# Clustered attention and two FFNs on one core: small attention steps rewritten to read PSUM, the planner's costs re-set, and the first transfers put in another order

## The chip, the cores and the metric

One core of one Trainium2 chip runs the whole program. The metric is device time in microseconds (us) of one execution, lower is better. A measurement of this kernel can tell about 1% (8 us) from no change.

## The reference

```python
def _attn_ref(q, k, v, centroids):              # B,H,S,D = 2,8,768,64; 16 clusters
    q_n = q / (norm(q) + 1e-06); k_n = ...; c_n = ...
    q_assign = argmax(einsum('bhsd,hcd->bhsc', q_n, c_n), axis=-1)   # k_assign alike
    mask = q_assign[:, :, :, None] == k_assign[:, :, None, :]
    scores = where(mask, scale * q @ k.T, -1000000000.0)
    scores = scores - max(scores, axis=-1, keepdims=True)
    attn = exp(scores); attn = attn / (sum(attn) + 1e-09)
    return attn @ v
# x = attention output as (1536 tokens, 512)
def _moe_ref(x, w_in, w_out, alpha):            # d_ff = 2048
    h = x @ w_in
    return (maximum(h, 0) + alpha * minimum(h, 0)) @ w_out
def _moe2_ref(x, w_in, w_out, a, b):
    h = x @ w_in
    P = a[0] + a[1]*h + a[2]*h**2 + a[3]*h**3
    Q = 1.0 + abs(b[0])*abs(h) + abs(b[1])*h**2
    return (P / (Q + 1e-6)) @ w_out
```

The FFN weights arrive as float64 and are rebuilt as float32 on the chip. A query whose cluster holds no key gets the mean of v.

## The kernel before

The attention works on 16 heads in 8 pairs. Everything is kept as two float32 or float16 parts, a high one and a remainder ("hi" and "lo"), so that the products are accurate.

For a pair, `ph_T` transposes q and k (L523; ACT writes hi, VectorE subtracts lo, L528 and L530), `ph_logits`, `ph_lt` and `ph_oht` find the cluster of each row and make a one-hot matrix (L592 writes it). `operands1` and `operands2` then copy the parts of a head into the operand tiles `op1` and `op2` by DMA (L615, L618, L621 and L629, L633).

For a head, `max_chunk` forms nine 512-column score tiles in PSUM (L659), each reduced to row maxima on VectorE (L665). `m_chain` takes the maximum of the parts (L674), makes `nm` from it (L677, VectorE, SBUF to SBUF), flags rows without a key (`nh`, L679, GpSimd), transposes nm (L682), negates it (L684) and sends it by DMA as a row of `op1` (L686). `st_chunk` computes the scores again with that row subtracted (L705, L706) and ACT takes the exponential (L710). `p_split` turns the result into float16: hi is a cast (the helper `copy`, L414 on ACT or L416 on GpSimd), lo is a subtraction of two SBUF tiles (L722). `pv_tile` multiplies by v (L790 to L792, 18 matmuls for a tile of 128 queries, 6 tiles for a head), and `pv_fin` divides: four small or middle VectorE steps L807, L809, L810 and L812, and L814, which overwrites rows without a key with the mean of v, from SBUF into SBUF. `x_T` transposes the pair's output into x.

`v_split` does a pair's v once: a scale from the sum of squares (L733, L740, L745 to L755), the mean of v (reduce L737, L742), then hi (L765, L767) and lo (L770).

The FFNs follow in 96 steps of 12 matmuls of 512 columns for h (L1033) and 12 for y (L1102). `w_prep` loads and rebuilds weights (L973, L976, L996 to L1018; L1009 and L1016 on GpSimd). Its first weights are prepared while the attention still runs.

The order of all instructions is written by a planner, `Sched`. Each `op` has a list of alternatives (engine, cost in us, a bias, and for some a hold of a port that the planner treats as shared by VectorE and GpSimd), the tiles it reads and writes, a priority `SC.t`, and an earliest time `after`. `run` walks in planned time, always starts what can start first, and picks the alternative with the earliest planned end plus bias. `BIAS["DVE"]` is added to every VectorE alternative of an op that has more than one. The planned order becomes the order in each engine's in-order queue; all DMAs go through SyncE's queue. `nb(n)` is the planned duration of a transfer of n bytes, `first` the earliest planned times of the first loads. The lo of `p_split`, L722, has these two alternatives, and in the kernel before all 96 went to GpSimd:

```python
        op([but(dve2(S), -0.1715), but(pool2(S), -0.0503)],
           lambda e: e.tensor_sub(pt_.v[:, 1, :], src(), pt_.v[:, 0, :]),
```

With S = 768 `dve2` costs 0.866 and `pool2` 1.783.

Of the kernel before, what the change touches and what calls it, by code (L numbers as in the profile page):

```python
# [253 lines left out]
def clustered_attention__then__ffn_prelu__then__ffn_rational(  # L254
# [471 lines left out]
    vmean, vinv = {}, {}  # L726

    def v_split(j):
        raw, d = raws["v", j], vs[j % 2]
        am, vr, vm_, ps = SC.buf("am"), SC.buf("vr"), SC.buf("vmean"), SC.buf("o", "v")  # L730
        junk = SC.buf("junk")
        for h in range(2):
            op(act_s(384, 2), lambda e, h=h: e.activation(  # L733
                junk.v.rearrange("p (t d) -> p t d", t=T), raw.v[:, h], ACTF.Square,
                accum_out=vr.v[:, 2 * D + h:2 * D + h + 1]),
               r=[raw], w=[(vr, h), junk])
# [5 lines left out]
        op([(ACT, 0.17), (DVE, 0.2)], lambda e: (e.mul(vm_.v, ps.v[:, :2 * D], 1.0 / S)  # L742
           if e is nc.scalar else e.tensor_scalar(vm_.v, ps.v[:, :2 * D], 1.0 / S, None,
                                                  op0=ALU.mult)), r=[ps], w=[vm_])
        op((DVE, 0.1), lambda e: e.tensor_scalar(  # L745
            am.v[:, 2:4], ps.v[:, 2 * D:2 * D + 2], 2.0 ** -120, None, op0=ALU.max),
           r=[ps], w=[am])
        op((DVE, 0.1), lambda e: e.tensor_scalar(
            am.v[:, 2:4].bitcast(U32), am.v[:, 2:4].bitcast(U32), 1, 0x7F800000,
            op0=ALU.logical_shift_right, op1=ALU.bitwise_and), r=[am], w=[am])  # L750
# [1 line left out]
        op((POOL, 0.17), lambda e: e.tensor_scalar(
            am.v[:, 2:4], am.v[:, 2:4], 2.0 ** 50, 0.0, op0=ALU.mult, op1=ALU.add),
           r=[am], w=[am])
        op((POOL, 0.17), lambda e: e.tensor_scalar(  # L755
            am.v[:, 0:2], am.v[:, 0:2], 2.0 ** -50, 0.0, op0=ALU.mult, op1=ALU.add),
           r=[am], w=[am])
# [415 lines left out]
```

## Time and profile before

| | us |
|---|---|
| median of 3 runs | 821.07 (818.24 to 824.56) |
| the profiled execution, its own time | 825.44 |
| its span, first to last instruction | 823.4 |
| mean granted TensorE clock | 0.965 |
| busy: TensorE 768.9 (93%), VectorE 606.6 (74%), ScalarE 570.4 (69%), GpSimd 596.2 (72%) | |

In the rows PE is TensorE (PEld its weight loads), DVE VectorE, ACT ScalarE, POOL GpSimd, SPq the queue of SyncE, from which DMAs are issued. "a<-b" says what is written and what is read; arenas are the two large SBUF areas, `bank` is PSUM. A time in brackets with an arrow is idle time of the engine before the instruction and what ended it. A busy PE is not PE at its peak, since matmuls are pipelined.

### The profile page before, as it was taken

To read this page: it belongs to the slowest core of one execution; us is meant where nothing else is said; L and a number is where in the kernel's file an instruction comes from. 1 tells how busy PE (TensorE), PEld (TensorE's weight loads), DVE (VectorE), ACT (ScalarE), POOL (GpSimd) and SP (SyncE) were. 2 spreads that over 40 slices of the span, in tenths; PEclk is the share of its full clock that TensorE was granted. 3 is DMA by queue.
4 is the path that set the end of the run, shared out by engine and by line. 5 is a ranking of instruction groups with operands and counts; after the bars stand their busy time and mean duration, and the time that the engine had idled before them with its cause. 6 is when DMAs were issued, how large, how long until landed. Compare 5 with 4: busy or idle time off the path is not lost.

```text
span 823.4 us, 13646 instructions
## 1 busy us (share of the span) xinstructions
PE 768.9 (93%) x5103; PEld 636.6 (77%) x5103; DVE 606.6 (74%) x884; ACT 570.4 (69%) x1002; POOL 596.2 (72%) x496
## 2 busy tenths in 40 slices
PE   7888888999878579999999999999999999999997
PEld 6667767878757458888888888888888888888885
DVE  5695979899786867865455365358889889987775
ACT  3377869888877757765564465579989788767662
POOL 4077659778677999987575476689889789877443
PEclk9888989999989889999999999999999999999999
DMA  8653737667435222333131032021111111000012
GB/s 166 138 102 84 154 72 167 129 132 165 109 70 168 86 95 81 111 117 102 52 103 52 30 99 78 26 67 62 52 42 61 52 51 52 1 0 1 2 52 102
DMA packets 57858, 67.56 MB, mean 82 GB/s; under 512 B 27232, under 2 KB 46272, under 8 KB 57792
## 3 DMA queue, kind: packets, MB, share of 16 engines
q1 hardware_dynamic: 57792, 66.69, 31.2%
q8 instruction: 40, 0.66, 0.3%
q14 instruction: 26, 0.21, 0.1%
HBM read 43.04 MB, written 3.15 MB: 56 GB/s over the span
## 4 chain that ended last, share of the span: by engine, by line
PE 61%; DVE 1%; POOL 1%; issue 1%; ACT 0%; DVEq 0%; POOLq 0%
PE bank L1102 31%; PE bank L1033 30%; DVE arena_p L1044 0%; POOL arena_p L1061 0%; POOL arena_r L1079 0%; POOL arena_p L722 0%; DVE arena_p L1121 0%; DVE rc L810 0%; PE bank L792 0%; DVE arena_p L1006 0%; PE bank L790 0%; PE bank L791 0%; PE bank L830 0%; DVE bank L1044 0%; ACT arena_r L414 0%
## 5 line engine op out<-in xcount | busy, mean ns | idle before, releaser
L1102 PE MATMUL bank<-arena_r 128*128 128x512 f32 x1152 | 278.5, 390 | 8.8 <-ACT arena_r L414 8.4
L1033 PE MATMUL bank<-x,arena_r 128*128 128x512 f32 x1152 | 278.5, 391 | 0.4 <-POOL arena_r L1016 0.4
L1102 PEld LDWEIGHTS bank<-arena_r 128*128 128x128 f32 x1152 | 216.3, 188 | 55.4 <-ACT arena_r L414 9.2
L1033 PEld LDWEIGHTS bank<-x,arena_r 128*128 128x128 f32 x1152 | 216.7, 188 | 46.1 <-POOL arena_r L1016 1.1
L722 POOL TENSOR_TENSOR arena_p<-arena_p 128x768 f16<-128x768 f32 x96 | 162.8, 1716 | 31.1 <-ACT arena_p L414 27.3
L1079 POOL TENSOR_TENSOR arena_r<-arena_p,arena_r 128x512 fp32r<-128x512 f32 x96 | 133.4, 1390 | 52.2 <-ACT arena_r L414 41.9
L414 ACT CAST arena_r<-arena_p 128x512 fp32r<-128x512 f32 x133 | 80.8, 620 | 48.8 <-DVE arena_p L1044 29.4
L665 DVE TENSOR_REDUCE mp<-bank 128x1 f32<-128x512 f32 x144 | 92.0, 680 | 25.9 <-PE bank L659 25.6
L1044 DVE SCALAR_TENSOR_TENSOR arena_p<-arena_p,nal 128x512 f32<-128x512 f32 x48 | 54.2, 1130 | 70.2 <-ACT arena_p L1047 70.1
L1016 POOL TENSOR_TENSOR arena_r<-arena_p,arena_r 128x512 fp32r<-128x512 f32 x64 | 88.6, 1388 | 19.4 <-ACT arena_r L414 18.6
L1009 POOL TENSOR_TENSOR arena_p<-arena_p 128x512 int32<-128x512 int32 x64 | 90.6, 1418 | 11.1 <-ACT arena_p L1002 7.1
L710 ACT ACTIVATE arena_p<-bank 128x512 f32<-128x512 f32 x144 | 79.7, 594 | 23.0 <-PE bank L706 14.6
L1004 DVE TENSOR_SCALAR arena_p<-arena_p 128x512 uint32<-128x512 uint32 x64 | 61.4, 961 | 41.3 <-ACT arena_p L996 41.3
L705 PE MATMUL bank<-arena_r 128*128 128x512 f32 x192 | 70.1, 382 | 14.2 <-DVE mp L665 6.0
L1061 POOL TENSOR_TENSOR arena_p<-arena_p 128x512 f32<-128x512 f32 x48 | 62.7, 1309 | 26.7 <-ACT arena_p L1058 26.6
L1006 DVE SCALAR_TENSOR_TENSOR arena_p<-arena_p 128x512 uint32<-128x512 uint32 x64 | 75.2, 1174 | 1.1
L414 ACT CAST arena_p<-arena_p 128x768 f16<-128x768 f32 x93 | 74.5, 838 | 0.3
L706 PE MATMUL bank<-arena_r 128*128 128x512 f32 x192 | 65.0, 352 | 0.0
L790 PE MATMUL bank<-arena_p 128*128 128x65 f16 x576 | 63.4, 199 | 1.1 <-DVE arena_p L812 1.1
L1044 DVE SCALAR_TENSOR_TENSOR arena_p<-arena_p,cq,bank 128x512 f32<-128x512 f32 x48 | 35.8, 745 | 38.9 <-ACT bank L1069 31.8
L792 PE MATMUL bank<-arena_p 128*128 128x65 f16 x576 | 62.5, 198 | 1.3 <-POOL arena_p L722 1.1
L791 PE MATMUL bank<-arena_p 128*128 128x64 f16 x576 | 62.7, 197 | 0.0
(121 smaller groups left out, 1247.2 us busy)
## 6 DMA issues: line engine op xcount, KB each, us to landing
arena_p<-in_moe_w_in SPq DMA_DIRECT2D x32, 512.0 KB, 3.6
arena_p<-in_moe_w_out SPq DMA_DIRECT2D x32, 512.0 KB
arena_r<-arena_r SPq DMA_DIRECT2D x24, 384.0 KB, 4.0
arena_r<-arena_r SPq DMA_DIRECT2D x24, 192.0 KB, 5.4
arena_p<-in_q SPq DMA_DIRECT2D x8, 384.0 KB, 5.3
arena_p<-in_k SPq DMA_DIRECT2D x8, 384.0 KB, 7.0
arena_r<-x SPq DMA_DIRECT2D x8, 384.0 KB, 9.6
arena_p<-in_v SPq DMA_DIRECT2D x8, 384.0 KB
```

The source lines that it names most:

```text
L414: e.copy(o_, i_)
L665: op(dvep(CH), lambda e: e.reduce_max(mp.v[:, n0:n0 + np_], ps.v.rearrange("p (a k) -> p a k", a=np_), axis=AX.X), r=[ps], w=[(mp, c)])
L705: e.matmul(o_, lhsT=b_.v[:, 1, ks], rhs=b_.v[:, 0, lo:hi], start=True, stop=False)
L710: op(act_p(CH), lambda e: e.activation(p32.v.rearrange("p a s -> p (a s)")[:, cc * CH:(cc + 1) * CH], ps.v, ACTF.Exp, scale=scale), r=[ps] ...
L722: lambda e: e.tensor_sub(pt_.v[:, 1, :], src(), pt_.v[:, 0, :]),
L1006: op(dve2(N), lambda e, d0=d0, hi=hi: e.scalar_tensor_tensor(u(d0), hi(), 0x80000000, u(d0), op0=ALU.bitwise_and, op1=ALU.bitwise_or), r=[ ...
L1009: op(pool2(N), lambda e, d0=d0, d1=d1: e.tensor_tensor(n32(d0), n32(d0), n32(d1), op=ALU.add), r=[d0, d1], w=[d0])
L1016: lambda e, wt=wt, pick=pick, src=src: e.tensor_tensor(pick(wt.v)[:, 1], src(), f32(pick(wt.v)[:, 0]), op=ALU.subtract),
L1033: e.matmul(ps.v, lhsT=wi.v[:, wi_, kk, :], rhs=x[kk][:, xi, cols], start=n == 0, stop=n == 3 * KD - 1)
L1044: lambda e: e.scalar_tensor_tensor(o_.v, a_.v, sc, b_.v, op0=p0, op1=p1))
L1079: op([dve2(N), pool2(N)], lambda e: e.tensor_tensor(gg.v[:, 1, :], G.v, f32(gg.v[:, 0, :]), op=ALU.subtract), r=[G, (gg, 0)], w=[(gg, 1)])
L1102: e.matmul(ps.v, lhsT=lhsT, rhs=rhs, start=first and wi_ == gi == 0, stop=last and gi == 1)
```

## The change

- `m_chain`: L677 and the tile nm go. The padding column that each tile's maxima get holds -BIG/2, so L674 itself gives the limited maximum; the transpose takes mx, and the constant is added where the transposed row is negated.
- `v_split`: the mean of v goes (L737, L742, L745); the scale comes from one VectorE step that reads PSUM, one on GpSimd and a reciprocal. Hi and lo are now made from a scaled copy of v that ACT writes to a PSUM bank: two writes to a bank, two copies to hi (ACT or VectorE), two VectorE subtractions PSUM minus SBUF for each pair.
- `pv_tile`: before a head's first tile 12 more matmuls (a constant matrix times v's hi and lo) put the sum of v in the same PSUM bank. `pv_fin`: rows without a key are overwritten in PSUM, before the division; L810 is joined to L807.
- First transfers: earliest planned times for the loads of q, k, v (`first`), for `operands2` of heads 0 and 1, and for three small loads of FFN constants.
- The planner: `BIAS["DVE"]` 1.8311 to 1.0, transfers at 280e3 bytes per us in place of 360e3, and longer costs for TensorE's operations.

```diff
-BIAS = {"DVE": 1.8311, "POOL": 0.0}
+BIAS = {"DVE": 1.0, "POOL": 0.0}
...
-    first = {("q", 2): 7.9688, ("k", 2): 7.9688, ("q", 3): 29.6134,
-             ("k", 3): 29.6134, ("v", 0): 20.0, ("v", 1): 22.6833}
+    first = {("k", 1): 9.0, ("q", 2): 34.0, ("k", 2): 36.0, ("q", 3): 44.0,
+             ("k", 3): 46.0, ("v", 0): 27.2, ("v", 1): 40.0}
...
-        return n / 360e3
+        return n / 280e3
...
+        late = (18.6, 27.0)[i] if i < 2 else 0.0
         op((DMA, nb(393216)), lambda e: e.dma_start(
             out=f32(a.v[0:64]), in_=f32(pt_.v[r, 0::3, :])),
-           r=pk_(pt_, "qh", "kl"), w=[(a, 0)])
+           r=pk_(pt_, "qh", "kl"), w=[(a, 0)], after=late)
...
-            mx.v, mp.v.rearrange("p (t a) -> p t a", a=2), axis=AX.X),
+            mx.v, mp.v.rearrange("p (t a) -> p t a", a=3), axis=AX.X),
            r=[(mp, c) for c in range(NCH)], w=[mx])
-        op((DVE, 0.07), lambda e: e.tensor_scalar(
-            nm.v, mx.v, -BIG / 2, LNP / scale, op0=ALU.max, op1=ALU.subtract), r=mk, w=[nm])
...
-        op((PE, 0.11), lambda e: e.transpose(ps.v[:T, :P], nm.v, idf), r=[nm], w=[ps])
+        op((PE, 0.11), lambda e: e.transpose(ps.v[:T, :P], mx.v, idf), r=[mx], w=[ps])
         op([(ACT, 0.16), (DVE, 0.2)], lambda e: (
-            e.mul(mt.v, ps.v[:T, :P], -1.0) if e is nc.scalar else
+            e.activation(mt.v, ps.v[:T, :P], ACTF.Copy, scale=-1.0, bias=LNP / scale)
...
-        op((DVE, 1.4), lambda e: e.reduce_sum(
-            vr.v[:, :2 * D].rearrange("p (h d) -> p h d", h=2),
-            raw.v.rearrange("p h t d -> p h d t"), axis=AX.X), r=[raw], w=[(vr, 2)])
...
-            op([act_s(384, 1), dve1(384), pool1(384, 1)], cvt, r=[raw, am], w=[(d, h, 1)])
-            op(dve2(384), lambda e, h=h, sc=sc, hi=hi, lo=lo: e.scalar_tensor_tensor(
-                lo(), raw.v[:, h], sc(), hi(), op0=ALU.mult, op1=ALU.subtract),
-               r=[raw, am, (d, h, 1)], w=[(d, h, 0)])
+            pv_ = SC.buf("S", "v")
+            pr = lambda pv_=pv_: pv_.v[:, :384].rearrange("p (t d) -> p t d", t=T)
+            op(act_s(384, 1), lambda e, h=h, sc=sc, pr=pr: e.activation(
+                pr(), raw.v[:, h], ACTF.Copy, scale=sc()), r=[raw, am], w=[pv_])
+            op([act_p(384), dvep(384)], lambda e, pr=pr, hi=hi: copy(e, hi(), pr()),
+               r=[pv_], w=[(d, h, 1)])
+            op(dvep(384), lambda e, pr=pr, hi=hi, lo=lo: e.tensor_tensor(
+                lo(), pr(), hi(), op=ALU.subtract), r=[pv_, (d, h, 1)], w=[(d, h, 0)])
...
+            def sums(e):
+                for kt in range(T):
+                    e.matmul(ps.v[:, 390:455], lhsT=level, rhs=d.v[:, e_, kt, 64:129],
+                             start=kt == 0, stop=False)
+                    e.matmul(ps.v[:, 390:454], lhsT=level, rhs=d.v[:, e_, kt, 0:64],
+                             start=False, stop=kt == T - 1)
...
-        op((DVE, 0.07), lambda e: e.tensor_scalar(rc.v, ps()[:, :, 64], PSC * 1e-9, None,
-                                                  op0=ALU.add), r=pk, w=[rc])
+        op(dvep(390), lambda e: e.copy_predicated(
+            ps(), nh.v.bitcast(U32).unsqueeze(2).to_broadcast([P, T, D + 1]),
+            ps_.v[:, 390:455].unsqueeze(1).to_broadcast([P, T, D + 1])),
+           r=[nh, (ps_, T)] + pk, w=pk)
+        op((DVE, 0.08), lambda e: e.tensor_scalar(
+            rc.v, ps()[:, :, 64], PSC * 1e-9, am.v[:, e_:e_ + 1], op0=ALU.add, op1=ALU.mult),
+           r=pk + [am], w=[rc])
         op((DVE, 0.11), lambda e: e.reciprocal(rc.v, rc.v), r=[rc], w=[rc])
-        op((DVE, 0.07), lambda e: e.tensor_scalar(rc.v, rc.v, am.v[:, 2 + e_:3 + e_], None,
-                                                  op0=ALU.mult), r=[rc, am], w=[rc])
...
-        op(dve2(384), lambda e: e.copy_predicated(
-            xn.v[:, :, e_, :], nh.v.bitcast(U32).unsqueeze(2).to_broadcast([P, T, D]),
-            vm_.v[:, e_ * D:(e_ + 1) * D].unsqueeze(1).to_broadcast([P, T, D])),
-           r=[nh, vm_, (xn, e_)], w=[(xn, e_)])
...
     op((DMA, 0.1), lambda e: e.dma_start(out=nal, in_=alpha.rearrange("(f p) -> p f", p=P)),
-       w=["nal"])
+       w=["nal"], after=40.0)
```

The loads of `nca` and `bab` get the same `after=40.0`. TensorE's planned costs go from 0.22 to 0.24 (max), 0.44 to 0.48 (st), 0.56 to 0.58 (pv), 2.6 to 2.724 (h), 0.434 and 0.217 to 0.454 and 0.227 (y).

## Rows read from the trace of the kernel before

**Rows 1.** The chain that ended last: start us, us, what; its first full pieces.

```profile
310.28 2.74 PE bank L1033 x12
...
317.10 2.72 PE bank L1102 x12
```

**Rows 2.** Busy time of each engine in four stretches (us from the span's start).

```profile
core 0: us, PE busy (x) PEld busy (x) DVE busy (x) ACT busy (x) POOL busy (x), PEclk, DMA share, GB/s
0.00:30.00 30.00, 23.06 (x204) 21.04 (x205) 14.71 (x36) 9.89 (x20) 9.66 (x39) 0.89 0.86 171
40.00:260.00 220.00, 195.30 (x2299) 163.82 (x2300) 186.68 (x331) 173.98 (x326) 159.83 (x129) 0.93 0.55 120
260.00:306.00 46.00, 29.72 (x301) 22.46 (x300) 34.53 (x34) 31.02 (x54) 44.80 (x29) 0.85 0.36 114
306.00:823.00 517.00, 511.62 (x2256) 422.59 (x2256) 361.93 (x469) 351.08 (x593) 381.67 (x299) 1.00 0.18 58
```

**Rows 3.** One line's instructions: duration ns min/median/max, first and last start us.

```profile
L674 DVE TENSOR_REDUCE mx<-mp x16: 149/158/168, 35.9 to 253.7; 128x6 f32<-128x12 f32 x16
...
L677 DVE TENSOR_SCALAR nm<-mx x16: 160/398/1620, 36.1 to 253.9; 128x6 f32<-128x6 f32 x16
...
L810 DVE TENSOR_SCALAR rc<-rc,am x16: 216/1036/1705, 68.9 to 302.7; 128x6 f32<-128x6 f32 x16
...
L814 DVE COPY_PREDICATED arena_p<-nh,arena_p x16: 577/592/2039, 72.6 to 305.7; 128x384 f32<-128x384 uint32 x16
...
L770 DVE SCALAR_TENSOR_TENSOR arena_p<-arena_p,am x16: 598/1166/2067, 42.8 to 245.8; 128x384 f16<-128x384 f32 x16
```

**Rows 4.** VectorE's groups from 0 to 306 us: busy us, mean ns; idle before.

```profile
L770 DVE SCALAR_TENSOR_TENSOR arena_p<-arena_p,am 128x384 f16<-128x384 f32 x16 | 20.0, 1263 | 0.0
L810 DVE TENSOR_SCALAR rc<-rc,am 128x6 f32<-128x6 f32 x16 | 15.1, 944 | 0.2
L814 DVE COPY_PREDICATED arena_p<-nh,arena_p 128x384 f32<-128x384 uint32 x16 | 15.0, 940 | 0.1
...
L737 DVE TENSOR_REDUCE arena_p<-arena_p 128x128 f32<-128x768 f32 x8 | 12.1, 1514 | 0.0
...
L677 DVE TENSOR_SCALAR nm<-mx 128x6 f32<-128x6 f32 x16 | 12.0, 750 | 0.0
...
L812 DVE TENSOR_TENSOR arena_p<-bank,rc 128x384 f32<-128x384 f32 x16 | 8.9, 558 | 0.4
L838 DVE TENSOR_TENSOR x<-bank,x 128x512 fp32r<-128x512 f32 x7 | 4.8, 688 | 3.2 <-ACT x L836 3.2
```

**Rows 5.** GpSimd's groups from 258 to 304 us.

```profile
L722 POOL TENSOR_TENSOR arena_p<-arena_p 128x768 f16<-128x768 f32 x12 | 22.0, 1854 | 0.1
L1009 POOL TENSOR_TENSOR arena_p<-arena_p 128x512 int32<-128x512 int32 x8 | 11.6, 1464 | 0.0
L1016 POOL TENSOR_TENSOR arena_r<-arena_p,arena_r 128x512 fp32r<-128x512 f32 x8 | 11.5, 1458 | 0.3
```

**Rows 6.** The groups of all engines, whole span: L722 and ACT's hi of v.

```profile
L722 POOL TENSOR_TENSOR arena_p<-arena_p 128x768 f16<-128x768 f32 x96 | 162.8, 1716 | 31.1 <-ACT arena_p L414 27.3 <-PE bank L659 2.1 <-PE bank L706 0.5
...
L765 ACT ACTIVATE arena_p<-arena_p,am 128x384 f16<-128x384 f32 x13 | 7.7, 612 | 0.0
```

**Rows 7.** SyncE's queue, the first transfers: issue start us, us.

```profile
4.71 2.18 SPq L949 DMA_DIRECT2D nal<-in_moe_alpha  x1
...
11.20 1.25 SPq L448 DMA_DIRECT2D arena_p<-in_q  x1
12.55 2.22 SPq L448 DMA_DIRECT2D arena_p<-in_k  x1
14.87 4.54 SPq L629 DMA_DIRECT2D arena_r<-x  x2
19.50 1.25 SPq L615 DMA_DIRECT2D arena_r<-x  x1
20.86 1.61 SPq L618 DMA_DIRECT2D arena_r<-arena_r  x1
```

**Rows 8.** Timeline: head 0's one-hot matrix is written, and its first score tile.

```profile
15.79 0.99 ACT L592 ACTIVATE arena_r<-bank,osc 64x768 fp32r<-64x768 bf16 x1 [2.60 <-PE bank L588]
...
29.90 0.94 PE L659 MATMUL bank<-arena_r 96*128 96x512 f32 x4 [1.21 <-DMA arena_r<-arena_r]
```

**Rows 9.** Timeline of PE: the first of 36 matmuls of two pv tiles, and what follows them.

```profile
129.89 0.20 PE L790 MATMUL bank<-arena_p 128*128 128x65 f16 x1
...
130.99 0.48 PE L705 MATMUL bank<-arena_r 128*128 128x512 f32 x1
```

More of the change, by code (lines that the diff above doesn't have):

```diff
@@ L418, in copy @@
             e.tensor_copy(o_, i_)
+    level = const.tile([P, P], F16, name="level")
+    nc.vector.memset(level, PSC)
     rev = const.tile([P, C], BF16, name="rev")
@@ L634, in operands2 @@
                 out=f32(a.v[64:128, n]), in_=f32(pt_.v[r, 2 - n])),
-               r=pk_(pt_, w_), w=[(a, 1 + n)])
+               r=pk_(pt_, w_), w=[(a, 1 + n)], after=late)
     small = {}
-    for tag, n, w_, dt in (("lmx", 2, 4 * T, F32), ("lmw", 2, 4 * T, BF16), ("mx", 3, T, F32), ("mp", 2, 2 * T, F32),
-                           ("nh", 3, T, F32), ("nm", 2, T, F32), ("rc", 2, T, F32),
+    for tag, n, w_, dt in (("lmx", 2, 4 * T, F32), ("lmw", 2, 4 * T, BF16), ("mx", 3, T, F32), ("mp", 2, 3 * T, F32),
+                           ("nh", 3, T, F32), ("rc", 2, T, F32),
                            ("am", 3, 4, F32)):
@@ L646, in clustered_attention__then__ffn_prelu__then__ffn_rational @@
     nohas = {}
+    for s in SC.slots["mp"]:
+        nc.vector.memset(s.view.rearrange("p (t a) -> p t a", a=3)[:, :, 2], -BIG / 2)
     maxparts = {}
@@ L734, in v_split @@
                 junk.v.rearrange("p (t d) -> p t d", t=T), raw.v[:, h], ACTF.Square,
-                accum_out=vr.v[:, 2 * D + h:2 * D + h + 1]),
-               r=[raw], w=[(vr, h), junk])
-        op((DVE, 1.4), lambda e: e.reduce_sum(
-            vr.v[:, :2 * D].rearrange("p (h d) -> p h d", h=2),
-            raw.v.rearrange("p h t d -> p h d t"), axis=AX.X), r=[raw], w=[(vr, 2)])
-        op((PE, 0.3), lambda e: e.matmul(ps.v[:, :2 * D + 2], lhsT=ones, rhs=vr.v, start=True,
-                                         stop=True), r=[(vr, i) for i in range(3)], w=[ps])
@@ L742, in v_split @@
[L742 to L750, printed above, removed]
@@ L751, in v_split @@
-        op((DVE, 0.1), lambda e: e.reciprocal(am.v[:, 0:2], am.v[:, 2:4]), r=[am], w=[am])
[L752 to L757, printed above, removed]
+                accum_out=vr.v[:, h:h + 1]), r=[raw], w=[(vr, h), junk])
+        op((PE, 0.22), lambda e: e.matmul(ps.v[:, :2], lhsT=ones, rhs=vr.v, start=True,
+                                          stop=True), r=[(vr, i) for i in range(2)], w=[ps])
@@ L758, in v_split @@
+        op((DVE, 0.08), lambda e: e.tensor_scalar(
+            am.v[:, 2:4].bitcast(U32), ps.v[:, :2].bitcast(U32), 1, 0x7F800000,
+            op0=ALU.logical_shift_right, op1=ALU.bitwise_and), r=[ps], w=[am])
+        op((POOL, 0.19), lambda e: e.tensor_scalar(
+            am.v[:, 2:4], am.v[:, 2:4], 2.0 ** -124, 2.0 ** 50, op0=ALU.max, op1=ALU.mult),
+           r=[am], w=[am])
+        op((DVE, 0.1), lambda e: e.reciprocal(am.v[:, 0:2], am.v[:, 2:4]), r=[am], w=[am])
         for h in range(2):
@@ L781, in pv_tile @@
         ps, d = pvps[i], vs[j % 2]
+        if t == 0:
+            def sums(e):
[4 more added lines that the diff above has]
+                             start=False, stop=kt == T - 1)
+            op((PE, 0.36), sums, r=[(d, e_, 0), (d, e_, 1), (d, "one")], w=[(ps, T)])
         qs = slice(t * P, (t + 1) * P)
@@ L949, in clustered_attention__then__ffn_prelu__then__ffn_rational @@
     op((DMA, 0.1), lambda e: e.dma_start(out=nal, in_=alpha.rearrange("(f p) -> p f", p=P)),
-       w=["nal"])
+       w=["nal"], after=40.0)
     op((DMA, 0.1), lambda e: e.dma_start(out=nca, in_=ca.unsqueeze(0).to_broadcast([P, 4])),
-       w=["nca"])
+       w=["nca"], after=40.0)
     op((DMA, 0.1), lambda e: e.dma_start(out=bab, in_=cb.unsqueeze(0).to_broadcast([P, 2])),
-       w=["bab"])
+       w=["bab"], after=40.0)
     op((POOL, 0.2), lambda e: e.tensor_scalar(nal, nal, -1.0, None, op0=ALU.mult),
```

47 lines of the change are left out of this document (22 added, 25 removed).

## Prediction, made before the changed kernel was run

> **What bounds the kernel now.** I read the chain that ended last first, then the busy time by stretches, then VectorE's and GpSimd's groups, then the first 30 us.
>
> The chain is nothing but FFN matmuls from 307 us on: 12 matmuls in 2.72 us, h and y in turn [rows 1], 0.227 us for one. There are 192 such dozens, 522 us, and from 306 us on PE is busy 511.6 of 517 us at a clock of 1.00 [rows 2]. Nothing in the change shortens an FFN matmul, so the end moves by as much as the moment at which the FFN gets going. The question is how long the attention takes: 306 us.
>
> The attention has three stages. From 0 to 30 us DMA is busy 86% at 171 GB/s and the engines mostly wait. From 40 to 260 us the heads run: 15 periods between 35.9 and 253.7 us [rows 3], 14.5 us each. From 260 to 306 us GpSimd is busy 44.8 of 46 us and everybody else much less [rows 2].
>
> In the middle stage PE shows the most busy time (195 of 220 us), then VectorE (187, 85%), ScalarE (174), GpSimd (160) [rows 2]. PE's number flatters it: the matmuls of a head at the rate of rows 1 are 18 x 0.227 (L705, L706) + 9 x 0.227 (L659) + 108 x 0.031 (36 pv matmuls took 1.10 us [rows 9]) = 9.4 us, with some 2 us of transposes and logits 11.5 of the 14.5. So PE waits, and I take VectorE for the bound. Its rows say why: L677 and L810 handle 6 numbers per partition and take 0.16 and 0.22 us at best but 0.75 and 0.94 in the mean; L814 and L770 double from their best [rows 3, 4]. The worst values lie 1.46 to 1.49 us above the best, nearly one L722 (1.72 us [rows 6]): VectorE waits for a running GpSimd instruction. L812, which reads PSUM and one SBUF tile, takes 0.558 us always.
>
> **The change part by part.** All sums are against the profiled execution (825.4 us; span 823.4), 4.4 us above the median of 821.07; I carry the difference over to the median.
>
> *Small steps off SBUF pairs.* Busy time less count times best: L677 12.0 - 16 x 0.160 = 9.4, L810 15.1 - 16 x 0.216 = 11.6, L814 15.0 - 16 x 0.577 = 5.8, L770 20.0 - 16 x 0.598 = 10.4: 37.2 us of waiting goes. Of own work L677 (2.6), L810 (3.5) and the reduce L737 (12.1) go: 18.2. The new overwrite in PSUM and the new subtraction for v's lo I price like L812 (0.558 for 384 elements), about what L814 and L770 take at best; the trace has no overwrite in PSUM, so its bounds are 0.558 and the 0.940 of now, 6 us over 16. VectorE loses 55 us, at least 49.
>
> The Trainium skill (SBUF — State Buffer, Who interferes with whom) says that a VectorE instruction with two SBUF inputs contends with a GpSimd instruction that reads SBUF, that one with at most one SBUF input outside the two-port modes does not, and that the later one waits for the whole of the other. The trace agrees: L812 has no spread, L770 has 1.5 us. By that rule the overwrite with only its mask in SBUF doesn't wait and the sum is 55; without it, 49. The same rule speaks against the lower VectorE bias, since the lo of the exponentials is such a pair: it is the mechanism of the third rival below.
>
> *The lower bias.* L722 may go to VectorE. The planned ends are 0.866 - 0.1715 + 1.0 = 1.69 there and 1.783 - 0.0503 = 1.73 on GpSimd, so of two free engines VectorE is now taken by a hair; before it needed GpSimd to be 0.79 us later. Price of one on VectorE: L770's best 0.598 for 384 elements, plus 384 more at (688 - 558)/128 = 1.02 ns [rows 4] = 0.99, plus a wait between nothing and L770's mean wait of 0.67. I take half, 1.32. How many go can't be seen in the trace; between 0 and 96, 0 to 158 us. VectorE is planned nearly full, so I take 20: +26 us, and GpSimd loses 34. Copies of v's hi on VectorE: 0 to 16 x 0.56; I take four, +2. Net for VectorE: -55 + 28 = -27, of which 85% (-23) in the middle stage.
>
> *What that is worth from 40 to 260 us.* If VectorE stays the bound at its 85%, 187 - 23 = 164 needs 193 us: -27. But ScalarE gets two more passes for each half of v (16 x about 1.1 us at L765's 0.61 and a bit less for a copy from PSUM, less L765's 7.7 us [rows 6]), 174 + 10 = 184, and would at 85% need 216: -4. It can give casts to the relieved GpSimd. I take -13, nearer the middle than an end since no row shows the new balance.
>
> *PE's sums of v.* 12 matmuls a head at 0.031: 0.37 x 16 = 5.9 us. PE has idle time, so between 0 and 5.9; I take +2. The longer planned costs move only the order: 0.
>
> *The first transfers.* Head 0's one-hot matrix is written at 16.8 us; its DMA (L618) is issued at 20.86 and the first score tile waits for it until 29.90 [rows 7, 8]. Ahead of it stand pair 2's q and k and two of `operands2`, 4 x 393216 bytes; at 171 GB/s 9.2 us. They go behind it: the tile starts near 20.7. Not all is won, since pair 2's preparation lay in that idle time: three subtractions like L838's (0.69) and four steps like L812 = 4.3 us on VectorE now fall among the heads. -9.2 + 4.3 = -5; bounds -9.2 and 0. `nal` and the two loads after it (2.18 us of issue for the first [rows 7]) move to planned 40 us, where on SyncE's queue head 0's and 1's rows (L686), one-hot matrices and pair 2's loads may stand behind them: 0 to +5; I take +1. Pair 2's transposes could wait for their late loads, on PE's in-order queue; before head 4 needs them there are 40 us, 0.
>
> *From 260 to 306 us.* 12 L722 and 16 weight steps of 1.46 us fill GpSimd [rows 5]. VectorE is busy 34.5 of 46, partly waiting. If three of these go over, 5 us of GpSimd's go: I take -4, bounds 0 and -9.
>
> *The FFN.* Weight and g steps may go to VectorE, too, at 70% there (361.9 of 517 [rows 2]): 0. Without this cover a gap of 1 us at each of 96 steps would be 96 us.
>
> Sum: -13 + 2 - 5 + 1 - 4 = -19. From the median: 802 us.
>
> **The rivals.**
>
> 1. *The bound passes on at once* to ScalarE (184 us of work) and PE: the middle stage gains 4, the start 4, the tail 2, less 1: -9, 812 us. For it: ScalarE's 79% is near VectorE's 85%. Against: it has casts to give away.
> 2. *Everything comes.* The middle -27, the start -9.2, the tail -9: -45, 776 us. Against: three engines at 73 to 85% would have to fit together without loss.
> 3. *VectorE takes too many of the 96 lo's.* Each is a pair of SBUF tiles: it waits for GpSimd and holds GpSimd off. From 55 / 1.32 = 42 on VectorE has more to do than before. With 50 at 1.5 us, +75 + 2 - 55 = +22, 19 in the middle: 206 / 0.85 = 242 us, +22; less 9 for start and tail: +13, 834 us, slower. For it: the bias lets VectorE win a tie. Against: a VectorE that is planned full loses most ties.
> 4. *The freed time is filled again*, with 35 to 40 lo's: the steps no longer wait, as the change says, and the heads take as long as now. Start and tail 4: 817 us.
>
> **How the numbers follow.** Forecast 0.50, rival 1 0.20, rival 2 0.08, rival 3 0.11, rival 4 0.11. About 1% (8 us) can be told from no change; faster is below 813. The forecast lies there nearly whole (0.48), rival 1 a little over half (0.12), rival 2 whole: 0.68. Within 1%: 0.02 + 0.08 + 0.11 = 0.21, slower 0.11. The range: down to 784, leaving out most of rival 2, up to 822, leaving out rival 3. The forecast's own is 790 to 812.
>
> **What would show it.** L674 comes 16 times at about 13.6 us instead of 14.5 and the first time near 27 us, not 36. The first L659 starts near 21. L677, L737, L742 and L745 are gone; the overwrite, the joined division step and v's lo show no spread between best and worst. Some 20 of the 96 lo's stand on VectorE at 1.0 to 2.6 us; GpSimd's busy time from the start to the FFN falls by 30. The FFN still takes 2.72 us for each dozen from its start to the end. I am wrong if VectorE's share in the heads isn't lower, if the heads take over 14.3 us, or if gaps appear in the FFN's dozens.

## The result and the profile after

The changed kernel takes 795.90 us in the median (793.82 to 797.74, 4 runs), the kernel before beside it 822.72: a ratio of 0.9681 [0.9629, 0.9733]. That is 26.2 us by the ratio, where 19 were forecast. The profiled executions say the same: 797.74 us after, 825.44 before, spans of 796.0 and 823.4.

Two starts cut every execution here into three pieces: L674, the maximum of a head's parts, starts 16 times, and its first and last start stand in [rows 3]. **First** is the time to the first start, **heads** the 15 periods between the two, **rest** what is left of the span. The rest is the last head's remainder and the FFN, and since a dozen of FFN matmuls takes 2.72 us before and after, a change of the rest is one of the stage between the last maximum and the FFN. The same line is L678 after. One line's instructions in the changed kernel, in the columns of [rows 3]:

```profile
L678 DVE TENSOR_REDUCE mx<-mp x16: 155/166/173, 26.7 to 235.3; 128x6 f32<-128x18 f32 x16
...
L808 DVE TENSOR_SCALAR rc<-bank,am x16: 208/224/225, 64.3 to 270.4; 128x6 f32<-128x6 f32 x16
...
L804 DVE COPY_PREDICATED bank<-nh,bank x16: 554/560/570, 60.6 to 269.8; 128x390 f32<-128x390 uint32 x16
...
L759 DVE TENSOR_TENSOR arena_p<-bank,arena_p x16: 547/550/559, 42.0 to 231.9; 128x384 f16<-128x384 f32 x16
...
L726 POOL TENSOR_TENSOR arena_p<-arena_p x66: 1638/1656/2372, 34.6 to 263.4; 128x768 f16<-128x768 f32 x66
L726 DVE TENSOR_TENSOR arena_p<-arena_p x30: 946/972/1935, 38.7 to 261.4; 128x768 f16<-128x768 f32 x30
```

First: 26.7 us, it was 35.9. Heads: 208.6, it was 217.8, so a period of 13.91 for 14.52. Rest: 796.0 - 235.3 = 560.7, it was 569.7. So 9.2, 9.2 and 9.0 us, 27.4 in all. The three steps that answer to L810, L814 and L770 no longer differ between best and worst: L808 takes 0.21 to 0.23 us (L810: 0.22 to 1.71), L804 0.55 to 0.57 (L814: 0.58 to 2.04), L759 0.55 to 0.56 (L770: 0.60 to 2.07). Of the 96 lo's 30 are on VectorE.

Busy time by stretches in the changed kernel, as [rows 2]; the cuts stand where the stages now end:

```profile
core 0: us, PE busy (x) PEld busy (x) DVE busy (x) ACT busy (x) POOL busy (x), PEclk, DMA share, GB/s
0.00:30.00 30.00, 25.20 (x218) 21.07 (x218) 19.48 (x50) 8.34 (x17) 9.34 (x36) 0.99 0.58 128
40.00:235.00 195.00, 184.46 (x2338) 158.13 (x2339) 160.59 (x296) 153.83 (x301) 141.57 (x117) 0.96 0.62 135
235.00:279.00 44.00, 35.04 (x454) 28.21 (x453) 38.02 (x46) 35.42 (x64) 40.04 (x26) 0.96 0.39 120
279.00:796.00 517.00, 510.98 (x2251) 421.72 (x2249) 375.54 (x470) 356.07 (x599) 384.18 (x293) 1.00 0.19 60
```

The last stretch is as long as before and as full of PE. In the heads VectorE is busy 82% (85% in [rows 2]), ScalarE 79, GpSimd 73; TensorE is now at 95%, where it was at 89. The chain that ended last shows the FFN's rate, as in [rows 1]:

```profile
277.38 2.72 PE bank L1029 x12
...
283.28 2.72 PE bank L1098 x12
```

VectorE's and GpSimd's groups from 0 to 279 us: busy us, mean ns, idle before.

```profile
L726 DVE TENSOR_TENSOR arena_p<-arena_p 128x768 f16<-128x768 f32 x30 | 35.0, 1167 | 10.8 <-ACT arena_p L414 6.9 <-POOL arena_p L416 3.8
...
L804 DVE COPY_PREDICATED bank<-nh,bank 128x390 f32<-128x390 uint32 x16 | 9.0, 562 | 5.5 <-PE bank L789 5.5
...
L759 DVE TENSOR_TENSOR arena_p<-bank,arena_p 128x384 f16<-128x384 f32 x16 | 8.2, 552 | 1.6 <-ACT arena_p L414 1.5
...
L726 POOL TENSOR_TENSOR arena_p<-arena_p 128x768 f16<-128x768 f32 x66 | 115.3, 1755 | 18.7 <-ACT arena_p L414 15.1 <-PE bank L684 1.5
...
L416 POOL TENSOR_SCALAR arena_p<-arena_p 128x768 f16<-128x768 f32 x31 | 27.3, 885 | 35.9 <-ACT arena_p L714 31.9 <-DMA arena_p<-in_v 2.5 <-PE bank L710 1.1
```

VectorE lost 12.0 + 15.1 + 12.1 us of steps that went, 15.0 - 9.0 at the overwrite and 20.0 - 8.2 at v's lo [rows 4]: 57 us. It took over 35.0 us of lo's. GpSimd lost 162.8 - 115.3 = 47.5 us of lo's [rows 6] and has now 31 casts of the exponentials, 27.3 us, which ScalarE gave away (it had 3 before).

### The profile page after: what moved, and what is told of

Same layout as the page of the kernel before. It is cut to its first block, busy times and chain, and to the rows that moved or that the text cites. A ratio compares the mean times of both kernels' runs of the same rounds, so it can differ in the third digit from the quotient of the medians.

```text
span 796.0 us, 13977 instructions
## 1 busy us (share of the span) xinstructions
PE 765.4 (96%) x5295; PEld 636.0 (80%) x5295; DVE 599.4 (75%) x871; ACT 560.3 (70%) x991; POOL 579.7 (73%) x475
## 4 chain that ended last, share of the span: by engine, by line
PE 84%; DVE 6%; DMA 5%; ACT 2%; POOL 1%; issue 1%; SPq 1%; DVEq 0%; ACTq 0%; POOLq 0%
PE bank L1029 32%; PE bank L1098 32%; PE bank L709 3%; PE bank L664 3%; PE bank L710 3%; DMA arena_r<-arena_r 2%; PE bank L787 2%; PE bank L552 2%; DVE mp L670 2%; PE bank L789 2%; PE bank L788 2%; DMA arena_p<-in_v 2%; PE bank L525 1%; DMA arena_p<-in_k 1%; DVE arena_p L726 1%
## 5 line engine op out<-in xcount | busy, mean ns | idle before, releaser
L1075 POOL TENSOR_TENSOR arena_r<-arena_p,arena_r 128x512 fp32r<-128x512 f32 x96 | 132.9, 1385 | 38.6 <-ACT arena_r L414 19.8
L726 POOL TENSOR_TENSOR arena_p<-arena_p 128x768 f16<-128x768 f32 x66 | 115.3, 1755 | 18.7 <-ACT arena_p L414 15.1
L414 ACT CAST arena_r<-arena_p 128x512 fp32r<-128x512 f32 x137 | 83.4, 621 | 44.7 <-DVE arena_p L1040 28.1
L1005 POOL TENSOR_TENSOR arena_p<-arena_p 128x512 int32<-128x512 int32 x64 | 93.8, 1468 | 27.1 <-ACT arena_p L998 15.9
L1012 POOL TENSOR_TENSOR arena_r<-arena_p,arena_r 128x512 fp32r<-128x512 f32 x64 | 92.5, 1447 | 13.0 <-ACT arena_r L414 12.5
L1000 DVE TENSOR_SCALAR arena_p<-arena_p 128x512 uint32<-128x512 uint32 x64 | 64.3, 1004 | 38.7 <-ACT arena_p L992 38.7
L1002 DVE SCALAR_TENSOR_TENSOR arena_p<-arena_p 128x512 uint32<-128x512 uint32 x64 | 84.1, 1315 | 1.5
L1040 DVE SCALAR_TENSOR_TENSOR arena_p<-arena_p,cq,bank 128x512 f32<-128x512 f32 x48 | 35.7, 744 | 41.8 <-ACT bank L1065 36.1
L664 PE MATMUL bank<-arena_r 96*128 96x512 f32 x192 | 53.1, 372 | 7.9 <-DMA arena_r<-arena_r 3.5
```

Source lines behind the costliest of these rows:

```text
L414: e.copy(o_, i_)
L1002: op(dve2(N), lambda e, d0=d0, hi=hi: e.scalar_tensor_tensor(u(d0), hi(), 0x80000000, u(d0), op0=ALU.bitwise_and, op1=ALU.bitwise_or), r=[ ...
L1005: op(pool2(N), lambda e, d0=d0, d1=d1: e.tensor_tensor(n32(d0), n32(d0), n32(d1), op=ALU.add), r=[d0, d1], w=[d0])
L1012: lambda e, wt=wt, pick=pick, src=src: e.tensor_tensor(pick(wt.v)[:, 1], src(), f32(pick(wt.v)[:, 0]), op=ALU.subtract),
L1040: lambda e: e.scalar_tensor_tensor(o_.v, a_.v, sc, b_.v, op0=p0, op1=p1))
L1075: op([dve2(N), pool2(N)], lambda e: e.tensor_tensor(gg.v[:, 1, :], G.v, f32(gg.v[:, 0, :]), op=ALU.subtract), r=[G, (gg, 0)], w=[(gg, 1)])
```

## The experiments

My theory behind the forecast was: the small steps carry most of the gain, by ending VectorE's waits for GpSimd; the bias adds a little; the first transfers add some 5 us; the planned costs add nothing. The rivals: the new bound eats the steps' gain; lo's on VectorE cost more than they bring; the start's gain is hidden or paid back. This table holds all runs in the three pieces (from the two starts and the span, as above; us of the profiled execution). Medians are of 4 to 10 runs, beside 822.1 to 823.5 of the kernel before; two kernels ran once, with a profile, and have no ratio. The pieces are those of one execution of each kernel, and the executions of one kernel lie 1 to 7 us apart here (those of the kernel before up to 11): a difference of a few us in one piece can be chance.

| kernel | median | ratio to before | first | heads | rest | lo's on VectorE |
|---|---|---|---|---|---|---|
| before | 822.72 | 1 | 35.9 | 217.8 | 569.7 | 0 |
| changed | 795.90 | 0.9681 [0.9629, 0.9733] | 26.7 | 208.6 | 560.7 | 30 |
| steps_alone | 811.23 | 0.9883 [0.9863, 0.9903] | 36.8 | 204.2 | 568.9 | 0 |
| bias_alone | 819.34 | 0.9959 [0.9939, 0.9979] | 34.8 | 214.4 | 569.2 | 20 |
| transfers_alone | 817.88 | 0.9940 [0.9916, 0.9963] | 29.3 | 216.8 | 573.6 | 0 |
| costs_alone | 825.61 | 1.0057 [1.0035, 1.0080] | 36.1 | 217.3 | 572.4 | 0 |
| no_steps | 808.75 | 0.9836 [0.9793, 0.9879] | 27.3 | 210.5 | 569.7 | 22 |
| no_bias | 802.35 | 0.9758 [0.9716, 0.9800] | 26.6 | 207.2 | 566.9 | 0 |
| no_transfers | 817.44 | 0.9926 [0.9898, 0.9955] | 35.6 | 220.6 | 559.7 | 33 |
| no_costs | 800.59 | 0.9737 [0.9680, 0.9795] | 28.2 | 207.8 | 563.1 | 30 |
| steps_bias | 795.21 | 0.9663 [0.9640, 0.9686] | 34.5 | 198.2 | 561.8 | 30 |
| bias_06 | 813.91 | 0.9886 [0.9857, 0.9914] | 26.8 | 225.8 | 561.3 | 72 |
| before_lo_vector | 845.45, one run | | 34.7 | 241.4 | 567.6 | 96 |
| after_lo_vector | 835.41, one run | | 26.8 | 244.8 | 562.0 | 96 |

**The steps alone.** The kernel before with the change of `m_chain`, `v_split` and `pv_tile`, and nothing else of it.

```diff
-BIAS = {"DVE": 1.0, "POOL": 0.0}
+BIAS = {"DVE": 1.8311, "POOL": 0.0}
...
-        return n / 280e3
+        return n / 360e3
```

(against the changed kernel; `first`, `after` and TensorE's costs go back likewise)

> The kernel before with the rewritten attention steps alone (m_chain, v_split, the sums of v, the overwrite in PSUM); bias, first transfers and planned costs stay as before. Main theory (VectorE's waits behind GpSimd bind the heads): L674's period falls from 14.5 us towards 13.7, no wait in the small steps, and the time falls by 8 to 16 us, with few or none of the lo's on VectorE. Rival A (the gain comes from the lo's that leave GpSimd): under 4 us. Rival B (any new order moves the time by as much): anything, and the four parts don't add up to 27 us.

Measured: 0.9883. The heads are 13.6 us shorter, a period of 13.61, and first and rest stay within 1 us. Its stretches, heads and then the stage up to the FFN:

```profile
core 0: us, PE busy (x) PEld busy (x) DVE busy (x) ACT busy (x) POOL busy (x), PEclk, DMA share, GB/s
40.00:241.00 201.00, 185.73 (x2329) 159.02 (x2329) 143.30 (x281) 168.71 (x319) 156.40 (x121) 0.96 0.59 131
241.00:284.00 43.00, 33.04 (x334) 27.31 (x335) 23.86 (x30) 29.49 (x53) 39.38 (x29) 0.80 0.29 86
```

VectorE fell to 143.3 of 201 us, 71%, ScalarE rose to 84%. So the steps free VectorE and shorten the heads by far less than VectorE was freed: the bound passed on, as the first rival has it. To which engine, this run doesn't tell, since its chain doesn't reach back into the heads. From 241 us on GpSimd is busy 39.4 of 43: the steps don't touch what fills that stage.

**The bias alone.**

```diff
-BIAS = {"DVE": 1.8311, "POOL": 0.0}
+BIAS = {"DVE": 1.0, "POOL": 0.0}
```

> The kernel before with VectorE's bias at 1.0 alone. Main theory: some 20 to 35 lo's go to VectorE, which has no room for them (+25 to +45 us of its work, its small steps still wait); the heads get longer by 5 us or more, the tail from 260 us shorter by about as much; total -5 to +5 us. Rival A: 12 us faster or more.

Measured: 0.9959, 20 lo's on VectorE, heads 3.4 us shorter, rest unchanged. I had expected longer heads and a shorter rest, and neither came. In the old kernel, where VectorE is 85% busy, the lower bias is worth 0.2 to 0.6%.

**Steps and bias**, neither transfers nor planned costs: steps_alone with the one line of bias_alone.

> The kernel before with the attention steps and the bias changed, and with the first transfers and planned costs as before. It tells whether the 21 us that the first transfers are worth in the changed kernel are theirs. Theory: no, they hold an accident of the order (38 us between two L678 where 13 to 22 are usual) that the new planned costs make with the old first transfers; without these costs there is no such gap, the end of the attention is as short as in the changed kernel, and only the 9 us of the start are missing: 803 to 808 us. Rival: the old first transfers stall the heads in any order: 813 or more.

Measured: 0.9663, the whole gain of the changed kernel (0.9681), 8 us below what I expected. The two edits save 13.5 and 5.0 us of span alone and 28.9 together (9.6, 3.4 and 27.8 by the ratios). Against steps_alone the heads lose another 6.0 us and the rest 7.1.

**The bias back in the changed kernel**

```diff
-BIAS = {"DVE": 1.0, "POOL": 0.0}
+BIAS = {"DVE": 1.8311, "POOL": 0.0}
```

> The changed kernel with VectorE's bias back at 1.8311. Theory now: the heads are bound by VectorE's waits, the end of the attention by GpSimd, and the lower bias pays only where the rewritten steps have made room on VectorE. Then all or nearly all lo's are on GpSimd again, the heads stay at 13.6 to 13.9 us, and the stretch from the last L678 to the FFN goes from 33 back to some 41 us: 800 to 806 us. Rival: the shorter end comes with the new order whatever the bias: 794 to 798.

Measured: 802.35 us; its runs (801.34 to 802.52) all lie above those of the changed kernel (793.82 to 797.74), though the intervals of the two ratios overlap. The heads are not longer than the changed kernel's (207.2 for 208.6), but the rest is, by 6.2 us. GpSimd's row of lo's from the last maximum to the FFN, first in the changed kernel (235 to 279 us), with VectorE's of the same time:

```profile
L726 POOL TENSOR_TENSOR arena_p<-arena_p 128x768 f16<-128x768 f32 x7 | 13.5, 1923 | 0.1
...
L726 DVE TENSOR_TENSOR arena_p<-arena_p 128x768 f16<-128x768 f32 x6 | 6.7, 1110 | 0.0
```

and without the bias (234 to 283 us), with the stretches of the heads and of that stage, in which GpSimd is busy 48.2 of 49 us:

```profile
L726 POOL TENSOR_TENSOR arena_p<-arena_p 128x768 f16<-128x768 f32 x14 | 24.7, 1792 | 0.9 <-POOL arena_p L726 0.8
```

```profile
core 0: us, PE busy (x) PEld busy (x) DVE busy (x) ACT busy (x) POOL busy (x), PEclk, DMA share, GB/s
40.00:234.00 194.00, 182.60 (x2338) 155.73 (x2339) 142.13 (x281) 164.67 (x316) 154.93 (x122) 0.98 0.66 142
234.00:283.00 49.00, 36.48 (x454) 30.35 (x452) 28.52 (x33) 36.52 (x65) 48.22 (x34) 0.90 0.31 96
```

The bias takes 11.2 us of lo's from GpSimd, just where GpSimd is the last to finish, and the rest shrinks by 6.2. In the heads ScalarE is busy 85% without the bias (164.7 of 194 us) and 79% with it, and the heads are as short either way. The granted clock of that stage differs, too (0.90 and 0.96); no run separates its share.

**The steps back in the changed kernel**: the old `m_chain`, `v_split` and `pv_tile` with everything else of the change.

> The changed kernel with the attention steps as before (bias, first transfers and planned costs as changed). Theory: heads at 14.3 us or more, a full VectorE can't help GpSimd, the last stretch stays near 41 us, only the start is won: 811 to 818 us. Rival (the steps matter little, the bias and the order do it): 802 or less.

Measured: 0.9836, less lost than I expected. The rest is back at 569.7, the value of before, though 22 lo's are on VectorE. With bias_alone, no_bias and steps_alone this closes the square: a rest of 563.1 or less stands only in kernels that have the steps and lo's on VectorE. The heads are 1.9 us longer than the changed kernel's, where the steps alone had made them 13.6 shorter: what the steps are worth there hangs on the rest of the order.

What binds the heads can be read from the chain that ended last, since it reaches back through them in these two kernels. Its shares of the span, by engine, in the changed kernel and then with the old steps:

```profile
PE 84%; DVE 6%; DMA 5%; ACT 2%; POOL 1%; issue 1%; SPq 1%; DVEq 0%; ACTq 0%; POOLq 0%
```

```profile
PE 75%; DVE 16%; POOL 4%; issue 2%; ACT 2%; DMA 1%; SPq 0%; DVEq 0%; POOLq 0%; ACTq 0%
```

Between the first and the last maximum VectorE holds 117 us of it with the old steps and 22 with the new, TensorE 85 and 139, DMAs none and 28, ScalarE 7 and 12. So the steps take the bound from VectorE, and it goes to TensorE, not to ScalarE. From the last maximum to the FFN GpSimd holds 22 us of it with the old steps and 4 in the changed kernel.

**The first transfers alone**: the hunks of `first`, `late` and `after=40.0` on the kernel before.

> The kernel before with the first transfers' new earliest times alone. Main theory: the first score tile starts at 20 to 21 us instead of 29.9, but VectorE, the bound of the heads, gets pair 2's preparation among them; of the 9 us some 5 reach the end (-3 to -8 us). Against it: 0 to -2 us if the heads are bound from the first one on by work that was there already; -9 if the start is won whole.

Measured: 0.9940, about the 5 us of the forecast, but of another make: first is 6.6 us earlier, heads 1.0 shorter, rest 3.9 longer. The profiled execution took 821.47 us, 3.6 above the median, so the longer rest may be chance.

**The planned costs alone**

```diff
-        return n / 360e3
+        return n / 280e3
...
-        op((PE, 2.6), mm, r=[(wi, 0), (wi, 1)] + [
+        op((PE, 2.724), mm, r=[(wi, 0), (wi, 1)] + [
```

(and TensorE's other costs)

> The kernel before with the planner's longer costs for TensorE and slower transfers alone. Main theory: only the order moves, -4 to +4 us. Rival B: 8 us or more either way.

Measured: 1.0057, 4.7 us slower, a little more than I expected, 2.7 us of it in the rest. The same edit taken back in the changed kernel:

> The changed kernel with the planned costs of TensorE and of transfers as before. Theory: only the order moves; alone these costs made the kernel 4.7 us slower, here between -5 and +3 us: 791 to 799. Rival: the realistic costs are needed for the order at the start and at the end, 803 or more.

Measured: 0.9737, 800.59 us, above the 791 to 799 that I expected; its interval overlaps that of the changed kernel. So the costs are worth between nothing and a few us with the rest of the change, and lose 3 to 7 us without it.

These two edits touch nothing but the planner's order and its choice of engines, and they move the time by 4.7 us one way and the other. The four parts of the change alone come to 9.6 + 3.4 + 4.9 - 4.7 = 13.2 us by their ratios, half of the 26.2 of the whole. That was the sign I had set for rival B of the first experiment, that any new order moves the time by as much. It holds for the small effects: one of 3 to 7 us can't be put down to one edit. Against it for the large ones stand the chains: of the kernels with the old steps, those whose chains reach back through the heads have VectorE in them for 67 us and more (transfers_alone, bias_alone, no_steps, before_lo_vector); those with the new steps and a bias of 1.0 have it for 29 at most.

**The first transfers back in the changed kernel**

> The changed kernel with the first transfers as before. Theory: L664 starts near 30 us instead of 20.6, the heads win back the 4 us of pair 2's preparation: 799 to 803 us. Rival 1: the start counts whole, 804 to 807. Rival 2: it counts for nothing, 795 to 797.

Measured: 817.44 us, some 15 more than I expected, and in the heads: a period of 14.71, longer than before. One gap makes most of it, 38 us between two maxima. From 60 to 80 us VectorE, ScalarE and GpSimd are busy 31 to 63% and DMA 15%; TensorE shows 86%, with 176 matmuls where 20 us of these heads have 217 in the mean:

```profile
66.17 0.16 DVE L677 TENSOR_REDUCE mx<-mp 128x6 f32<-128x18 f32 x1
...
104.36 0.16 DVE L677 TENSOR_REDUCE mx<-mp 128x6 f32<-128x18 f32 x1
```

```profile
core 0: us, PE busy (x) PEld busy (x) DVE busy (x) ACT busy (x) POOL busy (x), PEclk, DMA share, GB/s
60.00:80.00 20.00, 17.19 (x176) 14.55 (x174) 12.50 (x20) 8.84 (x20) 6.29 (x6) 0.86 0.15 37
```

Read alone this run would make the first transfers worth 21 us. But steps_bias lacks them as well, has no such gap, and runs at 795.2. What stands there is a bad order that the new costs make together with the old transfers. SyncE's queue serves head 2's row and the next matrices late there (two DMAs of L689 occupy it from 68.0 for 4.6 us, that of L617 comes at 77.3); which entry holds the others up I read from the queue and didn't isolate.

**All lo's on VectorE**, in the old kernel. If L810 and L770 wait for GpSimd, they must get faster although they are unchanged.

```diff
-        op([but(dve2(S), -0.1715), but(pool2(S), -0.0503)],
+        op([but(dve2(S), -0.1715)],
```

> The kernel before with all 96 lo's (L722) on VectorE, so that GpSimd has little to do among the heads. Theory (the small steps wait for a running GpSimd instruction that reads SBUF): L810 falls from 0.94 to 0.25 us in the mean, L677 from 0.75 to 0.2, L770 from 1.26 to 0.7, while they still work on SBUF pairs; a lo takes 1.0 us; VectorE has -35 + 96 x 1.0 = +61 us: 840 to 870 us in all. Rival (the small steps are slow by themselves, or wait for another thing): their means stay.

Measured: 845.45 us. VectorE's groups from 0 to 306 us, as [rows 4], and GpSimd's of the same time:

```profile
L722 DVE TENSOR_TENSOR arena_p<-arena_p 128x768 f16<-128x768 f32 x94 | 97.0, 1055 | 2.5 <-POOL arena_p L416 2.1
...
L770 DVE SCALAR_TENSOR_TENSOR arena_p<-arena_p,am 128x384 f16<-128x384 f32 x16 | 10.0, 640 | 0.0
...
L810 DVE TENSOR_SCALAR rc<-rc,am 128x6 f32<-128x6 f32 x15 | 5.4, 362 | 0.1
```

```profile
L679 POOL TENSOR_SCALAR nh<-mx 128x6 f32<-128x6 f32 x16 | 11.6, 724 | 44.9 <-DVE arena_p L814 22.7 <-DVE mx L674 21.8
```

L770 went from 1263 to 640 ns in the mean and L810 from 944 to 362, the same instructions on the same tiles, once GpSimd had no lo's. And GpSimd's small step L679, whose mean was 250 ns before, now takes 724: the wait goes to the other side. The time is worse all the same, for VectorE has 97 us of lo's more.

**All lo's on VectorE in the changed kernel**, the same edit.

> The changed kernel with all 96 lo's on VectorE: the third rival of the prediction at its end. Theory: 66 more at about 1.0 us make VectorE the bound, +66 us of work of which 10 to 15 us had room: the time is 825 to 850 us. Against the theory: under 805, VectorE then isn't what limits the heads.

Measured: 835.41 us, a period of 16.32, the longest of all.

**A lower bias still**, `BIAS = {"DVE": 0.6, ...}`.

> The changed kernel with VectorE's bias at 0.6. Theory: 40 to 50 lo's on VectorE, its share of the heads back at 87% or more, 796 to 803 us, so 1.0 is near the best. Rival: GpSimd at the end of the attention still sets the time, then 788 to 793.

Measured: 813.91, where I expected 796 to 803; 72 lo's on VectorE, not 40 to 50.

```profile
L726 DVE TENSOR_TENSOR arena_p<-arena_p x72: 936/948/2391, 38.9 to 278.6; 128x768 f16<-128x768 f32 x72
```

```profile
core 0: us, PE busy (x) PEld busy (x) DVE busy (x) ACT busy (x) POOL busy (x), PEclk, DMA share, GB/s
40.00:250.00 210.00, 190.08 (x2315) 160.40 (x2316) 192.20 (x333) 145.34 (x279) 99.45 (x100) 0.93 0.59 130
```

VectorE is at 92% in the heads, GpSimd at 47%. In the changed kernel 0, 30, 72 and 96 lo's on VectorE give 802.4, 795.9, 813.9 and 835.4 us. The rest hardly cares from 30 on (560.7, 561.3, 562.0); the heads pay. No run tells whether a number between 0 and 30, or a little above, is better still; none of these kernels beats the changed one beyond the intervals, and steps_bias equals it.

## Why the prediction was right

**The bound.** Right where it matters: the FFN keeps its 2.72 us, and the end moves with the attention. VectorE's waits for GpSimd were real and are gone from the rewritten steps (the 30 lo's still wait, 35.0 - 30 x 0.946 = 6.6 us); before_lo_vector shows that they came with GpSimd's work, not with the instructions.

**The steps.** 55 us of VectorE time were forecast to go, 57 went. The overwrite in PSUM, for which no row stood, takes 0.56 us, the lower bound that I chose. The prediction calls all these steps SBUF pairs, but L677 reads one SBUF tile only; it waited all the same. By the Trainium skill (SBUF — State Buffer, Who interferes with whom) a VectorE instruction with at most one SBUF input, outside the two-port modes, doesn't contend with GpSimd; L804, L808 and L759 agree, with 0.02 us between best and worst.

**The heads.** -13 for the steps is what steps_alone measured, 13.6; that it came so near is luck, for I had taken a value between -27 and -4, and with the other edits in place the steps are worth 1.9 there (no_steps). The net forecast of the heads was -13 + 2 + 4.3 + 1 = -5.7; 9.2 came. By that sum the period is 14.1 us, not the 13.6 that I named as a sign, which counts the -13 alone; 13.91 was measured. ScalarE is relieved as I said it could be, by 31 casts that GpSimd takes; the lower bias makes the room for them (ScalarE is busy 168.7 of 201 us with the steps alone, 153.8 of 195 in the changed kernel). But no run shows that this shortens the heads: no_bias has 14 casts on GpSimd and heads of 207.2. TensorE, whose share of the heads I called flattering, is where the chain lies now. VectorE's relief in sum was 20.8 us up to the FFN ((606.6 - 361.9) - (599.4 - 375.5)), for 27 forecast; GpSimd's is (596.2 - 381.7) - (579.7 - 384.2) = 19, for 30.

**The lo's.** 30, not 20, at 1.17 us in the mean, not 1.32; the median of 0.97 is the work alone, for which I had 0.99. The 1.17 is this order's: steps_bias has 30 lo's, too, at 1.29 in the mean.

```profile
L725 DVE TENSOR_TENSOR arena_p<-arena_p x30: 940/1082/2391, 50.7 to 263.0; 128x768 f16<-128x768 f32 x30
```

The third rival didn't come, but its shape did: bias_06 and after_lo_vector go up. With 72 lo's the heads are 8.0 us longer than before, as its break-even of 42 has it; that the kernel is still faster than before (0.9886) it owes to the start and the rest. I had taken each lo dearer the more there are; that is wrong, it costs 1.14 us with 72 and 1.04 with 96. That GpSimd then has fewer instructions to wait for would explain it; no run shows it alone.

**From the last head to the FFN: the mis-sized step.** "If three of these go over, 5 us of GpSimd's go: I take -4." 9.0 went, the end of its bounds: six lo's run on VectorE there, not three, and the square of runs gives 6.2 to 7.1 us of it to the bias on top of the steps. The chain agrees: GpSimd holds 4 us of it there, 22 with the old steps. This term is 5 of the 8 us that the forecast lacks; the heads' 3.5 are the others.

**The first transfers.** First came 9.2 us earlier, as worked out from four transfers ahead of head 0's matrix. But that it is worth 5 us to the whole is not shown: steps_bias does without (and without the new costs) and ends at the same time, starting the heads 7.8 us later and spending 10.4 less in them. Nor is it shown to be worth nothing: no_bias and steps_alone differ by the same two edits, and there the kernel that has them is 8.9 us faster. Starts of the first six maxima, in the changed kernel:

```profile
26.66 0.17 DVE L678 TENSOR_REDUCE mx<-mp 128x6 f32<-128x18 f32 x1
34.37 0.17 DVE L678 TENSOR_REDUCE mx<-mp 128x6 f32<-128x18 f32 x1
48.71 0.17 DVE L678 TENSOR_REDUCE mx<-mp 128x6 f32<-128x18 f32 x1
63.66 0.15 DVE L678 TENSOR_REDUCE mx<-mp 128x6 f32<-128x18 f32 x1
80.02 0.17 DVE L678 TENSOR_REDUCE mx<-mp 128x6 f32<-128x18 f32 x1
92.79 0.17 DVE L678 TENSOR_REDUCE mx<-mp 128x6 f32<-128x18 f32 x1
```

and in steps_bias:

```profile
34.55 0.17 DVE L677 TENSOR_REDUCE mx<-mp 128x6 f32<-128x18 f32 x1
42.15 0.17 DVE L677 TENSOR_REDUCE mx<-mp 128x6 f32<-128x18 f32 x1
50.06 0.16 DVE L677 TENSOR_REDUCE mx<-mp 128x6 f32<-128x18 f32 x1
63.49 0.16 DVE L677 TENSOR_REDUCE mx<-mp 128x6 f32<-128x18 f32 x1
78.15 0.16 DVE L677 TENSOR_REDUCE mx<-mp 128x6 f32<-128x18 f32 x1
90.46 0.16 DVE L677 TENSOR_REDUCE mx<-mp 128x6 f32<-128x18 f32 x1
```

The lead is 7.9 us, 7.8, 1.35, and gone by the fourth maximum. So it is spent between 34 and 64 us. What I find there in the changed kernel is a VectorE that sits 4.1 us before v's first step, whose load was moved back, too:

```profile
38.61 0.16 DVE L742 TENSOR_SCALAR am<-bank 128x2 uint32<-128x2 uint32 x1 [4.07 <-PE bank L740]
```

and the three subtractions of pair 2's preparation, 2.0 us at 47.4 to 52.7 us, which steps_bias has at 21.6 to 28.1. The four other steps of that preparation, which I had priced along with them at 4.3 us, lie between 34 and 64 us in both kernels (the one on `lmx` at 49.6 and at 56.9). The two are 6.1 of the 8.1 us that are lost, but this is read from the traces; no run moved them singly.

**The small loads on SyncE's queue.** They take 0.90, 3.52 and 1.62 us of its time at 47.9 to 54.1 us, 6.0 together, where I had 2.18 for the first; what that costs the heads stays open, as no run moved them alone.

**The rivals.** The first (812) has the time of the steps alone (811.2), and the bound does pass on; but of the two engines that it names, ScalarE and TensorE, the chain of the changed kernel shows TensorE. The second (776) had start and rest right and the heads far too good: with -19.6 us in the heads steps_bias came nearest, without the start's gain. The fourth (817), freed time filled again, didn't come. Whether part of the gain is TensorE's clock stays open: the granted clock rose from 0.93 to 0.96 in the heads and from 0.85 to 0.96 up to the FFN, and no run holds it still. TensorE's busy time in the heads fell from 195.3 to 184.5 us with no fewer matmuls (2299 and 2338), and since the chain there now lies on TensorE, this rival can't be set aside.

## What to carry to other kernels

Look for tiny instructions whose mean is several times their best: the wait is there to be removed, and the sum of count times (mean less best) is what VectorE gets back, though not what the kernel gets. When an edit makes room on an engine, set the knob that shares work among engines anew together with it; each alone was worth 9.6 and 3.4 us here by the ratios, both 27.8. And judge an edit to a planned order by adding it as well as by removing it: taking the first transfers out cost 21 us, and a kernel that had neither them nor the new costs was as fast.

## What the runs showed of the hardware that I had not expected

The wait works in both directions. GpSimd's `nh`, six numbers per partition, has a median of 226 ns in the kernel before, 842 with all lo's on VectorE; the two rows one after the other:

```profile
L679 POOL TENSOR_SCALAR nh<-mx x16: 226/226/594, 36.2 to 257.2; 128x6 f32<-128x6 f32 x16
```

```profile
L679 POOL TENSOR_SCALAR nh<-mx x16: 229/842/1000, 34.9 to 285.2; 128x6 f32<-128x6 f32 x16
```

By the Trainium skill (SBUF — State Buffer, Who interferes with whom) the one that issues first holds the shared ports for its whole instruction; the extra 0.6 us, less than a lo's 0.95, fit that. How often it happens hangs on the order: in the changed kernel with all lo's on VectorE the median is 236 ns again, and the worst is 1001.

Among VectorE's own small steps in the kernel before only the scalar steps from SBUF to SBUF waited (L677, L810, and L748 in two of its eight times, 0.32 and 1.09 us where its best is 0.15); the maximum L674 and the reciprocal L809, from SBUF to SBUF with 0.149 to 0.168 and 0.174 to 0.194 us, never did. What sets them apart no run tells.
